# Banded attention and a leaky-relu MLP on one core: attention's products from the third batch on use TensorE's array in quarters, in one stretch a visit

## The chip, the core and the metric

The kernel runs on one core of a Trainium2 chip. The metric is the device time of one execution in microseconds (us). TensorE (PE) multiplies matrices into PSUM, which has eight banks of 512 fp32 columns on 128 rows; VectorE (DVE), ScalarE (ACT) and GpSimd (POOL) work on what is there and in SBUF; SyncE (SP) issues the loads.

## The reference

Attention over 8 batches, 8 heads, 576 tokens and 64 elements a head; heads 0 to 3 look back over 32 neighbours, heads 4 to 7 over 32 tokens at a distance of 4. Its output, as 4608 rows of 512, goes through an MLP:

```python
rel = pos[:, None] - pos[None, :]
mask_plain = (rel >= 0) & (rel < 32)
mask_dil = (rel >= 0) & (rel < 32 * 4) & (rel % 4 == 0)
scores = np.where(masks, q @ k.T / np.sqrt(64), -1e9)
attn = exp(scores - max); attn = attn / (attn.sum(-1) + 1e-9)
x = (attn @ v).transpose(0, 2, 1, 3).reshape(4608, 512)
h = x @ w_in                      # w_in is 512 x 2048
out = np.maximum(0.01 * h, h) @ w_out   # w_out is 2048 x 512
```

Inputs and the output are float32; the kernel's matrix operands are fp16.

## The kernel before

**The order of the work.** The kernel first lists tasks, each with an engine (or several to choose from), a duration, what it depends on and a priority. A planner lays them out engine by engine, goes backward over the result eight times to set priorities, and then adds to the priorities a table of numbers by task (NUDGE) and fixes some engines by hand (HAND). The instructions are emitted in the order that comes out. So a change to the tasks moves instructions on every engine, and what a row of an engine waits for is what the emitted order makes of it: each engine works through its own instructions in order, and semaphores hold one back until what it needs on another engine is done.

**Loading.** Query and key come in fp32, are cast to fp16 and turned, so that the 64 elements of a head lie on rows; two heads fill the 128 rows. Batches 0 and 1 (EARLY) are turned by TensorE (`turn`, L743, and `turn_rest` for the last 64 tokens) into PSUM and copied out. Batches 2 to 7 are turned by VectorE in 32x32 blocks (L708 to L735) into `turned`, and copied from there into `slots` by GpSimd, ScalarE or VectorE (`move`, L516 and L517).

**Attention.** A visit is a batch and a pair of heads; the order of pairs is VISITS = (2, 3, 0, 1), where 0 and 1 are plain and 2 and 3 are dilated. The keys of the two heads are interleaved on the 128 rows. A visit has two `unit`s. A unit is: scores, five products on the whole array (L899); Exp on ScalarE (L907); the mask as a multiply on VectorE (L911); from some batch on an add of overlapping parts (L932); sums of the exponentials, products with a block of ones (L924); values, five products (L918); 1/sum as Ln and Exp(-1 x) on ScalarE (L943, L945); and the multiply of values by it into `xt` on VectorE (L956). Scores, sums and values of a unit are three separate tasks of TensorE, and the order puts blocks of the MLP between them.

**The MLP.** `up` (L1057) makes one block of the hidden layer for 384 tokens, four products of 128x384 into one of the banks hps0 and hps1, and ScalarE's Prelu (L1073) takes it out. `up_pair` (L1091) does so for 192 tokens. The last three chunks of tokens use `ups7` (L1191), a scheme of seven products for eight. `down` (L1271) makes the first four output tiles; `group` (L1361, blocks of eight products 128x256, with sums on VectorE, L1347) makes the rest by seven products for eight, in the banks fps0, fps1 and tp, with evictions L1390 and L1392.

**PSUM.** Eight tiles of one bank each: tp, ops0, ops1, hps0, hps1, sps, fps0, fps1. An instruction on one bank is ordered only against what uses that bank.

Of the kernel before, what the change touches and what calls it, by code (L numbers as in the profile page):

```python
# [14 lines left out]
WIN = 32  # L15
# [3 lines left out]
WHEN = (3.92, 2.82, 39.64, 80.18, 115.4, 117.81, 161.72, 152.03)  # L19
# [3 lines left out]
ADDED = (2, 9)  # L23
LAPS = ("DVE", "POOL")
# [1643 lines left out]
```

## Time and profile before

| | before |
|---|---|
| median of 3 runs | 294.49 us (294.41 to 294.5) |
| span of the profiled execution | 292.5 us |
| time of the profiled execution beside its span | not listed |
| TensorE busy in the span | 285.2 us, 97% |
| VectorE, ScalarE, GpSimd busy | 226.8, 218.9, 121.2 us |
| share of TensorE in the chain that ended last | 93% |

A row of instructions reads: line, engine, operation, output and inputs, shape, then times in us. A group's row gives the count, the sum of the busy time in us and the mean of one in ns, then the idle time of the engine ahead of the group and what ended it. The records of TensorE overlap: a product's record lasts until its result is in PSUM, and the next one begins before that, so the time that a product costs is the spacing of the products, not the record.

### The profile page before, as it was taken

To read this page: it belongs to the slowest core of one execution; us is meant where nothing else is said; L and a number is where in the kernel's file an instruction comes from. 1 tells how busy PE (TensorE), PEld (TensorE's weight loads), DVE (VectorE), ACT (ScalarE), POOL (GpSimd) and SP (SyncE) were. 2 spreads that over 40 slices of the span, in tenths; PEclk is the share of its full clock that TensorE was granted. 3 is DMA by queue.
4 is the path that set the end of the run, shared out by engine and by line. 5 is a ranking of instruction groups with operands and counts; after the bars stand their busy time and mean duration, and the time that the engine had idled before them with its cause. 6 is when DMAs were issued, how large, how long until landed. Compare 5 with 4: busy or idle time off the path is not lost.

```text
span 292.5 us, 7626 instructions
## 1 busy us (share of the span) xinstructions
PE 285.2 (97%) x2924; PEld 226.4 (77%) x2924; DVE 226.8 (78%) x437; ACT 218.9 (75%) x483; POOL 121.2 (41%) x173
## 2 busy tenths in 40 slices
PE   6899999999999999999999999999999999999995
PEld 2567776776787788677777877887688999999985
DVE  7877588674799789858839889897878889678672
ACT  3997987589869966878888987888767966755522
POOL 5420452458537746964873774653425000000000
PEclk9999999999999999999999999999999999999999
DMA  7999999799898959999799798751101210121133
GB/s 244 267 389 396 395 377 224 150 168 218 142 188 185 179 144 174 191 168 208 197 170 160 180 205 151 195 134 59 36 2 36 75 38 0 38 74 36 38 109 110
DMA packets 156068, 47.15 MB, mean 161 GB/s; under 512 B 136832, under 2 KB 153344, under 8 KB 156032
## 3 DMA queue, kind: packets, MB, share of 16 engines
q1 hardware_dynamic: 155344, 46.04, 65.0%
q10 hardware_dynamic: 688, 0.63, 0.6%
q8 instruction: 23, 0.38, 0.5%
q14 instruction: 13, 0.11, 0.1%
HBM read 37.22 MB, written 9.44 MB: 160 GB/s over the span
## 4 chain that ended last, share of the span: by engine, by line
PE 93%; ACT 2%; DVE 2%; DMA 1%; issue 1%; ACTq 0%; DVEq 0%
PE hps L1057 27%; PE fps L1361 23%; PE tp L1361 9%; PE hps L1191 5%; PE fps L1271 4%; PE hps L1091 4%; PE ops L1191 3%; PE ops L918 3%; PE ops L899 2%; PE sps L899 2%; PE ops L924 2%; PE sps L1191 1%; DMA con<-consts 1%; PE sps L924 1%; PE ops L1361 1%; PE sps L918 1%
## 5 line engine op out<-in xcount | busy, mean ns | idle before, releaser
L1057 PE MATMUL hps<-xt,w_in 128*128 128x384 f16 x488 | 94.7, 325 | 0.0
L1361 PEld LDWEIGHTS <-gt 128*128 128x128 f16 x768 | 73.0, 98 | 9.8 <-DVE gt L1347 0.2
L1073 ACT ACTIVATE gt<-hps 128x384 f16<-128x384 f32 x122 | 59.1, 487 | 13.7 <-PE hps L1057 12.7
L1057 PEld LDWEIGHTS <-w_in 128*128 128x128 f16 x512 | 44.9, 98 | 21.3 <-issue 0.3
L505 POOL CAST slots<-vst 128x576 f16<-128x576 f32 x55 | 46.0, 861 | 22.7 <-DMA vst<-in_v_dram 5.6
L505 POOL CAST nat<-stg 128x576 f16<-128x576 f32 (+1 forms) x52 | 34.6, 687 | 48.6 <-DVE gt L1347 15.1
L1361 PE MATMUL fps<-w_out,gt 128*128 128x256 f16 x368 | 46.7, 272 | 0.0
L911 DVE TENSOR_TENSOR ee<-ee,con 128x384 f16<-128x384 f16 (+1 forms) x48 | 20.6, 430 | 15.3 <-ACT ee L907 14.9
L945 ACT ACTIVATE rc<-rc 128x288 f32<-128x288 f32 (+1 forms) x64 | 27.2, 436 | 1.1
L956 DVE TENSOR_TENSOR xt<-ops,rc 128x288 f16<-128x288 f32 (+2 forms) x44 | 19.3, 445 | 9.7 <-ACT rc L945 4.9
L516 ACT COPY slots<-turned 64x512 f16<-64x512 f16 (+1 forms) x30 | 23.8, 799 | 0.8 <-DVE turned L708 0.5
L1214 ACT ACTIVATE gt<-vst 128x384 f16<-128x384 f32 (+1 forms) x24 | 16.0, 684 | 8.0 <-DVE vst L1210 8.0
L899 PEld LDWEIGHTS <-slots 128*128 128x128 f16 x308 | 18.1, 98 | 4.7 <-DVE slots L517 0.4
L517 POOL COPY slots<-turned 64x576 f16<-64x576 f16 (+2 forms) x25 | 16.7, 675 | 11.2 <-ACT slots L516 3.5
L907 ACT ACTIVATE ee<-ops 128x416 f16<-128x416 f32 (+2 forms) x35 | 16.7, 487 | 3.6 <-PE ops L899 3.0
L918 PEld LDWEIGHTS <-slots 128*128 128x128 f16 x308 | 17.1, 97 | 2.8 <-ACT slots L504 0.6
L924 PEld LDWEIGHTS <-con 128*128 128x128 f16 x168 | 14.0, 97 | 5.9 <-issue 0.8
L708 DVE STREAM_TRANSPOSE turned<-nat 128x576 f16<-128x576 f16 x24 | 18.0, 759 | 0.1
L1390 ACT COPY stg<-fps 128x512 f32<-128x512 f32 (+1 forms) x20 | 10.4, 519 | 9.4 <-PE fps L1361 9.1
L907 ACT ACTIVATE ee<-sps 128x416 f16<-128x416 f32 (+2 forms) x29 | 14.4, 495 | 3.8 <-PE sps L899 2.7
L1347 DVE TENSOR_TENSOR gt<-gt 128x1024 f16<-128x1024 f16 x21 | 16.6, 789 | 0.3 <-PE fps L1361 0.2
L1191 PEld LDWEIGHTS <-w_in 128*128 128x128 f16 x192 | 16.2, 98 | 0.2
(158 smaller groups left out, 559.8 us busy)
## 6 DMA issues: line engine op xcount, KB each, us to landing
out_dram<-osb SPq DMA_DIRECT2D x32, 256.0 KB, 2.6
stg<-in_k_dram SPq DMA_DIRECT2D x48, 144.0 KB, 3.6
stg<-in_q_dram SPq DMA_DIRECT2D x48, 144.0 KB, 3.4
vst<-in_v_dram SPq DMA_DIRECT2D x16, 288.0 KB, 4.3
vst<-in_v_dram SPq DMA_DIRECT2D x32, 128.0 KB, 3.2
gt<-in_moe_w_in_dram SPq DMA_DIRECT2D x6, 512.0 KB, 6.8
stg<-in_q_dram SPq DMA_DIRECT2D x3, 512.0 KB, 6.9
stg<-in_k_dram SPq DMA_DIRECT2D x3, 512.0 KB, 9.1
```

The lines of the kernel that those rows point to most:

```text
L505: return ENG[e].tensor_copy(out=dst, in_=src)
L516: return nc.scalar.copy(out=dst, in_=src)
L899: nc.tensor.matmul(p_bank[:, c:c + w], slot(tn, KB + 128 * s, 0, 128, [1, 128]), slot(tn, qx, 0, 128, *qd), start=first or not by_pe, stop ...
L907: lambda e: nc.scalar.activation(out=et[:, 0:n], in_=p_bank[:, 0:n], func=AF.Exp, scale=SCALE), prio)
L911: lambda e: nc.vector.tensor_tensor(out=et[:, 0:n], in0=et[:, 0:n], in1=con[:, table:table + n], op=ALU.mult), prio,
L918: nc.tensor.matmul(at(dst, 0, 128, o, *od), lhs(s), et[:, c:c + w], start=i == 0, stop=i == len(steps) - 1, skip_group_check=True)
L924: nc.tensor.matmul(at(p_bank, 0, 128, o, *od), block_ones, at(et, 0, 128, c, *cd), start=i == 0, stop=i == len(rows) - 1, skip_group_check ...
L945: lambda e: nc.scalar.activation(out=rt, in_=rt, func=AF.Exp, scale=-1.0), prio)
L1057: nc.tensor.matmul(ht[:, 0:n], at(w_in, 0, 128, vi * DFF + j // 2 * 256 + j % 2, [2, 128]), at(xt[m % 2], 0, 128, vi * 1152 + x0 + x, [1, n]),
L1073: lambda e: nc.scalar.activation(out=gt[c % NG][:, j * n_c + x:j * n_c + x + n], in_=ht[:, 0:n], func=AF.Prelu, alpha=0.01),
L1191: nc.tensor.matmul(bk[:, n * i:n * i + n], w(v, 2 * z + i), x(v), start=first and i == 0 and v == 0, stop=i == 1 and v == 1, skip_group_ch ...
L1361: nc.tensor.matmul(bk[:, x:x + HN], tl[:, off + j * step:off + j * step + 128], rhs(j), start=first and x == 0 and j == 0, stop=j == HJ - ...
```

## The change

From the third batch (number 2) on, attention is made of bursts. A `burst(now, then, prio, lent)` is one task of TensorE: the sums and values of the visit `now`, then the scores of the next visit `then`. Every product uses a quarter of the array, 64 rows by 64 columns (`tile_position`); a step is four of them, one for each quarter, and the two row halves write different banks. A burst has four banks, `seats`: ops0, ops1, a lent one, and sps. The lent one is tp until the first `group` is made, then fps0 or fps1, by the roles that the groups so far leave to the two. There are 25 bursts, with 64 to 68 products each where both parts are present: 480 for scores, 480 for sums and 624 for values, in place of 612 on the whole array.

Behind a burst stand one Ln over ops1 and sps (576 columns, L1276) and one Exp(-1 x) (L1279) for the visit `now`; two multiplies into `xt` (L1293), the first of 128 columns over ops0 and the lent bank, the second of 448 over ops1 and sps; and for the visit `then` one Exp over ops0 and the lent bank (L1304; 2 x 448 or 2 x 384 columns) and one mask multiply (L1313). For such accesses to two banks PSUM is now one tile, `psum`, of 4096 columns, cut into the banks 0 to 7: tp, ops0, ops1, sps, hps0, hps1, fps0, fps1. `up` is now L1336 with its Prelu at L1352, and a product of `group` is L1639.

Other parts: batch 2 is loaded like the early ones and turned by TensorE (PACKED = 3; 36 products in the banks sps and ops0, L890 and L951); batches 3 to 7 are turned by VectorE straight into `slots`, keys no longer interleaved, so the copies out of `turned` are gone; the overlap adds are gone; the table of masks is smaller; the first of the last three chunks uses the same ring of banks as the other two; bursts are placed every 5.2 up blocks (PLACE, PACE); NUDGE now has a number for nearly every task, and HAND is longer.

Instructions before and after: TensorE 5850 and 7870 rows with weight loads, VectorE 438 and 374, ScalarE 487 and 345, GpSimd 177 and 115, SyncE 231 and 257.

```diff
-WHEN = (3.92, 2.82, 39.64, 80.18, 115.4, 117.81, 161.72, 152.03)
+WHEN = (3.92, 2.82)
-ADDED = (2, 9)
-LAPS = ("DVE", "POOL")
+PLACE = 4.0
+PACE = 5.2
+SWITCH = 0.2
...
-    EARLY = 2
+    EARLY, PACKED = 2, 3
...
-    def bank(name, dt=FP32):
-        return ps.tile([128, 512 if dt == FP32 else 1024], dt, name=name)
...
-    tpb = bank("tp", FP16)
-    tp32 = tpb.bitcast(FP32)
-    ops = [bank(f"ops{i}") for i in range(2)]
-    hps = [bank(f"hps{i}") for i in range(2)]
-    sps = bank("sps0")
-    fps = [bank(f"fps{i}") for i in range(2)]
+    psum = ps.tile([128, 4096], FP32, name="psum")
+    tp32, *ops, sps, hps0, hps1, fps0, fps1 = (psum[:, 512 * i:512 * i + 512] for i in range(8))
+    tpb, hps, fps = tp32.bitcast(FP16), [hps0, hps1], [fps0, fps1]
...
-        if b >= EARLY:
-            xn, x_old = ring("X", NX, x_users := [])
-            xk = turned[xn][:, 0:S]
-            tk = add("DVE", 0.68, [c_qk[1]] + x_old,
...
+        if b >= PACKED:
...
+            for o, x in ((0, 0), (1, KB)):
+                order = ([1, 144], [144, 4]) if dil and o == 0 else ([1, S],)
+                got.append(add("DVE", 0.68, [c_qk[o]] + old,
+                               lambda e, o=o, x=x, order=order: nc.vector.transpose(
+                                   slot(tn, x, 0, 128, *order), na[:, o * S:o * S + S]), prio))
+            n_users += got
+            q_ready[b, vi], k_ready[b, vi] = got[:1], got[1:]
...
+            q_bank = second_turn[vi] if b < EARLY else sps
...
-        summed = [t_m, t_e, t_id]
-        if added:
-            c0, d0, c1, d1, w = lap
-
...
+    def burst(now, then, prio, lent):
+
+        seats = [ops[0], ops[1], lent, sps]
+        room, mine = {}, {}
+        for bk in seats:
+            room[key(bk)], mine[key(bk)] = grab(bk)
+        if now is None:
+            for bk in seats[1::2]:
+                mine[key(bk)] += room[key(bk)]
+        jobs, deps, cols = [], sum(room.values(), []), 0
...
+        def product(bk, x, od, lhs, rhs, p, q, first, last):
+            p0, p1, q0, q1 = quarter(p, q)
+            jobs.append(lambda: nc.tensor.matmul(
+                at(bk, q0, q1, x, *od), lhs(p0, p1, q), rhs(p0, p1), start=first, stop=last,
+                skip_group_check=True, tile_position=(p0, q0)))
+
...
+            for n, two in enumerate(list(zip(sums_of(vi, 0), sums_of(vi, 1)))
+                                    + list(zip(values_of(vi, 0), values_of(vi, 1)))):
+                for p, (blk, c, w, dims, x, *part) in enumerate(two):
+                    if not part:
+                        bk, x, first = seats[2 * p + 1], 224 + x, n == 0
+                    elif part[0]:
+                        bk, x, first = seats[2 * p], 448 + x, part[0] == 1
+                    else:
+                        bk, first = seats[2 * p + 1], False
+
+                    def lhs(p0, p1, q, blk=blk, part=part):
+                        if not part:
+                            return con[p0:p1, M_ONE:M_ONE + 64]
+                        return slot(tn, VB + 128 * blk + 64 * q, p0, p1, [1, 64])
+
+                    for q in range(2):
+                        def rhs(p0, p1, q=q, c=c, w=w):
+                            o = 896 * en + 448 * q + c
+                            return e_all[p0:p1, o:o + w]
+                        product(bk, x, dims, lhs, rhs, p, q, first, True)
+            cols += 2 * (416 if vi < 2 else 384) + 30
+            deps = deps + [t_m, t_con[0]] + v_in[b, vi]
+        if then is not None:
...
+            for _, c, w, keys, asks in places(b2, v2):
+                for p in range(2):
+                    for q in range(2):
+                        def lhs(p0, p1, _, k=keys[q]):
+                            return slot(t2, KB + k[1], p0, p1, k[0])
+
+                        def rhs(p0, p1, a=asks[q]):
+                            return slot(t2, a[1], p0, p1, *a[0])
+                        product(seats[2 * p], c, [[1, w]], lhs, rhs, p, q, True, True)
...
+        t_b = add("PE", SWITCH + cols / 2400.0, deps, pe, prio, 0.0, "B")
...
+            t_l = add("ACT", 0.07 + S / 1200.0, [t_b] + r_old,
+                      lambda e: nc.scalar.activation(out=at(rt, 0, 128, 0, [288, 2], [1, 288]),
+                                                     in_=both(1, 224, None, [1, 288]), func=AF.Ln), prio)
+            t_r = add("ACT", 0.105 + S / 1200.0, [t_l],
+                      lambda e: nc.scalar.activation(out=rt, in_=rt, func=AF.Exp, scale=-1.0), prio)
+            x, xm = vi * 1152 + b % 2 * S, xt[b // 2 % 2]
...
+                    args = (at(xm, 0, 128, x + n0, [288, 2], [1, w]), both(i, 0 if i else 448, None, [1, w]),
+                            at(rt, 0, 128, n0, [288, 2], [1, w]))
...
+            for i, bk in enumerate(seats):
+                mine[key(bk)] += [t_l, ts[1]] if i % 2 else [ts[0]]
...
+        t_e = add("ACT", 0.07 + 2 * n / 1200.0, [t_b] + then[4][0],
+                  lambda e: nc.scalar.activation(out=at(et, 0, 128, 0, [448, 2], [1, n]),
+                                                 in_=bass.AP(tensor=seats[0].tensor, offset=seats[0].offset,
+                                                             ap=[list(seats[0].ap[0]), [
+                                                                 seats[2].offset - seats[0].offset, 2], [1, n]]),
+                                                 func=AF.Exp, scale=SCALE), prio)
+        mine[key(ops[0])].append(t_e)
...
-            ring5 = five if c > 9 else [hps[0], hps[1], ops[1]]
-            X, Y, Z = (ring5[(five_at[0] + i) % len(ring5)] for i in range(3))
+            X, Y, Z = (five[(five_at[0] + i) % len(five)] for i in range(3))
...
+    visits = [(b, vi) for b in range(EARLY, B) for vi in VISITS]
+    flow, lent = [0, None], [tp32]
+
+    def bursts(upto, prio):
+        while flow[0] <= len(visits) and PLACE + PACE * flow[0] <= upto:
+            k, then = flow[0], None
+            if k < len(visits):
...
+            flow[:] = k + 1, burst(flow[1], then, prio, lent[0])
...
+                lent[0] = trio[roles[0]]
```

What the order makes of it, first on TensorE, before, in the middle of the run. L918 are a unit's values, L1057 the blocks of `up`, L924 the unit's sums:

```order
L918 LDWEIGHTS slots [waits Pool_49]
L918 MATMUL sps_104<-ee_81,slots 128x96 [waits DVE_49]
...
L918 MATMUL sps_104<-ee_81,slots 128x2x16
L1057 LDWEIGHTS w_in
L1057 MATMUL hps_103<-xt_87,w_in 128x384 [waits Activation_49]
...
L1057 MATMUL hps_102<-xt_87,w_in 128x384 [waits Activation_49]
...
L924 LDWEIGHTS con
L924 MATMUL ops_101<-ee_81,con 128x2x96
```

Values stand ahead of two blocks of `up`, the sums behind them; each block waits for the Prelu that frees its own bank. On TensorE, after, the end of a burst (its last product is a score, 64x96), the `up` block behind it, and the first product of a `group`, which writes fps0:

```order
L1218 MATMUL psum<-slots 64x96
L1336 LDWEIGHTS w_in
L1336 MATMUL psum<-xt_79,w_in 128x384 [waits Activation_49]
L1336 LDWEIGHTS w_in
L1336 MATMUL psum<-xt_79,w_in 128x384
...
L1639 LDWEIGHTS pair_87
L1639 MATMUL psum<-wst_88,pair_87 128x256 [waits Activation_49]
L1639 LDWEIGHTS pair_87
L1639 MATMUL psum<-wst_88,pair_87 128x256
```

Sums, values and scores are now one stretch. The group's first product waits for ScalarE; it is the wide Exp (L1304) that stands first in the last piece below, which reads ops0 and fps1 and not fps0. On ScalarE, before, in the same part of the program, with Exps L907 of one bank, Prelus L1073, an eviction L1390 and the Ln and Exp(-1 x) of a unit:

```order
L907 ACTIVATE ee_81<-sps_104 128x416 [waits DVE_49,PE_49]
L1073 ACTIVATE gt_88<-hps_103 128x384 [waits PE_49]
L907 ACTIVATE ee_82<-ops_101 128x416 [waits DVE_49,PE_49]
L1390 COPY osb_91<-fps_105 128x512 [waits DMAHW6_49,PE_49]
L943 ACTIVATE rc_83<-sps_104 128x288 [waits PE_49]
L945 ACTIVATE rc_83<-rc_83 128x288 [waits Activation_49]
```

and after, with the wide Exp, the wide Ln and Exp(-1 x), and Prelus L1352:

```order
L1304 ACTIVATE ee<-psum 128x896 [waits DVE_49,PE_49]
L1352 ACTIVATE gt_80<-psum 128x384
L1276 ACTIVATE rc<-psum 128x576
L1668 COPY stg_68<-psum 128x512 [waits DMAHW0_49,DMAHW7_49,PE_49,Pool_49]
L1352 ACTIVATE gt_80<-psum 128x384 [waits PE_49]
L1279 ACTIVATE rc<-rc 128x576 [waits Activation_49]
```

This wide Exp reads ops0 and fps1. Of TensorE it waits for the last product of the `up` block behind the burst, the fourth L1336 of the piece above, which writes hps1; the Prelu behind the Exp waits for nothing more.

More of the change, by code (lines that the diff above doesn't have):

```diff
@@ L758, in turn @@
         after_q, after_k = ([tq], [tk]) if b == 0 else ([tq, tk], [tq, tk])
+        if b >= EARLY:
+            got = []
+            for o in range(2):
+                if not dil:
+                    dst = slot(tn, KB * o, 0, 128, [4, 128], [1, 4])
+                    src = at(bq, 0, 128, 512 * o, [1, 128], [128, 4])
+                else:
+                    dst = slot(tn, KB * o, 0, 128, [128 if o else 144, 4], [1, 128])
+                    src = at(bq, 0, 128, 512 * o, [128, 4], [1, 128])
+                got.append(move(dst, src, 512, after_q + old, prio, ("DVE", "ACT"), dil, bank_q))
+            q_users += got
+            q_ready[b, vi], k_ready[b, vi] = got[:1], got[1:]
+            return
         if dil:
@@ L826, in unit @@
         qr, kr = q_ready[b, vi], k_ready[b, vi]
-        added, nq, bias = b >= ADDED[dil], 288, []
+        nq, bias = 288, []
         if dil:
-            wide, run = ((96, 64), 128) if by_pe else ((96, 80), 144)
-            nq, n, steps = 2 * run, 2 * sum(wide) + 32 * (not by_pe), []
+            wide, run = (96, 64), 128
+            nq, n, steps = 2 * run, 2 * sum(wide), []
             for ab in range(2):
@@ L908, in unit @@
                                                  scale=SCALE), prio)
-        t_m = t_e if by_pe else add(
-            "DVE", 0.08 + n * 0.00052, [t_e, t_con[0]],
-            lambda e: nc.vector.tensor_tensor(out=et[:, 0:n], in0=et[:, 0:n],
-                                              in1=con[:, table:table + n], op=ALU.mult), prio,
-            lock=True)
         def second(dst, lhs):
@@ L1516, in attend @@
         else:
-            banks = dict.fromkeys(VISITS, [sps, ops[0]] if b == 7 and 9 in SEVEN else three)
+            banks = dict.fromkeys(VISITS, three)
         for n, vi in enumerate(VISITS):
@@ L1525 @@
     wide_banks = {2: fps[0], 3: fps[1], 4: tp32, 5: sps, 6: ops[0], 7: ops[1]}
+    visits = [(b, vi) for b in range(EARLY, B) for vi in VISITS]
[4 more added lines that the diff above has]
+            if k < len(visits):
+                b, vi = visits[k]
+                if vi == VISITS[0]:
+                    fetch(b, prio, 6.5)
+                if b < PACKED:
+                    if vi == VISITS[0]:
+                        turn_rest(b, prio)
+                    turn(b, vi, prio)
+                elif vi == VISITS[0]:
+                    for v in VISITS:
+                        turn(b, v, prio)
+                then = take(b, vi)
+            flow[:] = k + 1, burst(flow[1], then, prio, lent[0])
     def ups(c, x, n, batches, js=(0, NJ)):
@@ L1529, in ups @@
             for j in range(*js, 2):
+                if x:
+                    bursts(8 + j / 2, begins[c] + j * 1.3)
                 up_pair(c, j, x, n, batches, all_acts[c], hps[h_at[0] % 2])
@@ L1533, in ups @@
         for j in range(*js):
+            if c > 1:
+                bursts(16 * (c - 1) + j, begins[c] + j * 1.3)
             wide_j = c == 0 and j in wide_banks
@@ L1580 @@
             weight_sums()
-            half_free[0] = raw[0, "rest"][1] + raw[1, "rest"][1]
+            half_free[0] = raw[PACKED - 1, "rest"][1]
             part_free[0] = part_free[1] = rings["STG"][-1]
-        while n_g < len(groups) and groups[n_g][-1][0] < 3 * m + 3:
-            four = groups[n_g]
-            group(four, all_acts, begins[four[-1][0] + 1] + four[-1][1] * 2.0, n_g == len(groups) - 1)
-            n_g += 1
+        for c, batches in ((3 * m, [e]), (3 * m + 1, [e, o]), (3 * m + 2, [o])):
+            if c in SEVEN:
+                if c == SEVEN[0]:
+                    bursts(1e9, begins[c])
+                    in_sums()
+                ups7(c, batches, all_acts[c])
+            elif m:
+                ups(c, 0, 384, batches)
+            elif c == 2:
+                ups(2, 0, 384, [o])
+            while n_g < len(groups) and groups[n_g][-1][0] <= c and c > 1:
+                four = groups[n_g]
+                group(four, all_acts, begins[four[-1][0] + 1] + four[-1][1] * 2.0, n_g == len(groups) - 1)
+                lent[0] = trio[roles[0]]
+                n_g += 1
     order = plan.run()
@@ L1592 @@
     order.sort(key=lambda t: (t.start, t.n))
-    slow = next(t for t in order if t.eng == "POOL" and t.kind == "cast" and t in ups_at[0].deps)
+    slow = next((t for t in order if t.eng == "POOL" and t.kind == "cast" and t in ups_at[0].deps), None)
     kept = [t for t in order if t.eng == "ACT" and t.start < ups_at[1].start]
-    if slow.start < kept[-1].start:
+    if slow is not None and slow.start < kept[-1].start:
         slow.eng, slow.start = "ACT", kept[-1].start + 1e-4
```

309 lines of the change are left out of this document (174 added, 135 removed), and 294 rows, old and new, of the table NUDGE.

## The prediction

> **What bounds the kernel now.** I read the page first, then busy time by stretches, then the chain of work in the middle of the run, then groups of instructions by shape, and last the order of time where one engine hands to another. From the page:
>
> ```profile
> span 292.5 us, 7626 instructions
> ...
> PE 285.2 (97%) x2924; PEld 226.4 (77%) x2924; DVE 226.8 (78%) x437; ACT 218.9 (75%) x483; POOL 121.2 (41%) x173
> ...
> PE 93%; ACT 2%; DVE 2%; DMA 1%; issue 1%; ACTq 0%; DVEq 0%
> ```
>
> Stretches, with columns length, then busy time and count of TensorE, its weight loads, VectorE, ScalarE and GpSimd, then the granted clock:
>
> ```profile
> 0.00:16.00 16.00, 12.27 (x97) 6.83 (x98) 12.72 (x22) 10.84 (x23) 7.81 (x16) 1.00 0.89 261
> ...
> 87.75:117.00 29.25, 29.25 (x303) 23.29 (x302) 24.72 (x47) 23.58 (x53) 19.27 (x29) 1.00 0.86 170
> 175.50:204.75 29.25, 29.25 (x297) 22.98 (x295) 25.75 (x47) 24.52 (x55) 14.30 (x20) 1.00 0.58 135
> ```
>
> TensorE is the bound, and without slack: in the two middle stretches it is busy for all 29.25 us at a clock of 1.00, while no other engine passes 25.8. So each microsecond of work taken from TensorE shortens the run, each microsecond for which it stands still lengthens it, and the other engines matter only through the moments at which they let TensorE go on. The three timed runs have a median of 294.49 us; the profiled execution's own whole time is not listed. The median stands 2.0 us over its span; I take those 2.0 us as what lies around the span, unchanged, and set the differences below on 294.5. Under 0.2% (0.6 us) a measurement of this kernel can't tell from no change.
>
> **What attention costs TensorE before.** The chain of work from 142 to 152 us shows its pieces (start, time until TensorE could go on, line):
>
> ```profile
> 142.42 0.38 PE ops L899 x10
> 142.80 1.30 PE hps L1057 x8
> ...
> 145.16 0.66 PE hps L1057 x4
> 145.82 0.14 PE ops L924 x3
> ...
> 146.61 0.12 PE ops L924 x2
> 146.73 0.87 PE fps L1361 x8
> 147.61 0.19 PE ops L918 x5
> ...
> 150.80 0.17 PE ops L899 x5
> ...
> 151.63 0.17 PE sps L924 x3
> 151.80 0.18 PE ops L918 x5
> ```
>
> A visit is two units. A plain visit costs 0.38 for its two sets of scores, 0.19 + 0.18 for values and 0.14 + 0.12 for sums: 1.01 us. A dilated one costs twice 0.17 + 0.18 + 0.17: 1.04 us. Batches 2 to 7 have 12 visits of each kind, 12 x 1.01 + 12 x 1.04 = 24.6 us. This is all that the quarters can work on.
>
> **The products in quarters: 24.6 becomes 14.0, between 14.0 and 56.** No row shows a product on a quarter of the array. From below: the four products of a step run side by side, and a step costs what a whole-array product of the same width costs now. Sums, values and scores then take one pass of five steps a visit instead of two, and the values one or two short steps more. Short steps, from the order of time:
>
> ```profile
> 21.74 0.53 PE L997 MATMUL sps<-slots 128*128 128x16 f16 x14
> ```
>
> These 14 end 0.53 after the first begins; one is recorded at about 0.18, so the others follow at (0.53 - 0.18)/13 = 0.027. A plain visit is then 3 x 0.19 + 0.03 = 0.60, a dilated one 3 x 0.17 + 0.06 = 0.57, 24 of them 14.0 us. From above: nothing overlaps, four times as much, 56 us. I take 14.0, since the four products of a step stand next to each other, read and write different quarters, and the two row halves write different banks. The Trainium skill (TensorEngine Tiling (Array Packing), Key Properties) says that different tiles can load weights and multiply in parallel; no run shows that yet.
>
> **Changing the division: +5.0, between 0 and 8.** Each of the 25 bursts has whole-array products before and behind it, so the division changes 50 times. The nearest rows are the recorded time of a product against its spacing:
>
> ```profile
> L1057 PE MATMUL hps<-xt,w_in 128*128 128x384 f16 x448 | 86.1, 325 | 0.0
> ...
> L918 PE MATMUL ops<-ee,slots 128*128 128x96 f16 x108 | 11.0, 205 | 0.0
> ```
>
> A 96-wide product is recorded at 205 ns, and its five stand 0.04 apart, so 0.16 us passes between the moment when the next can follow and its end. A change costs between nothing and this, 0 to 8 us in all; with no nearer row I take 0.1, 5.0 us. The Trainium skill (same page and section) says that a change of tiling mode drains TensorE. By that rule it would be the whole 8, and the sum 3 us more.
>
> **Batch 2 turned by TensorE: +2.0.** 36 products of 128x128 are added. Four of these (L743) are recorded as 0.38 where one is about 0.22, so one takes (0.38 - 0.22)/3 = 0.055:
>
> ```profile
> 15.71 0.38 PE L743 MATMUL fps<-con,nat 128*128 128x128 f16 x4 [0.23 <-DVE slots L517]
> ```
>
> 36 x 0.055 = 2.0. TensorE's own work thus goes from 24.6 to 14.0 + 5.0 + 2.0 = 21.0: **-3.6 us**, between -8.6 (no cost of division) and, with that at 8, -0.6.
>
> **The wait that comes with it.** Before, scores, sums and values lie in eight separate bank tiles, and an instruction waits only for its own bank. Now PSUM is one tile, and an access to two banks is ordered against everything between its first and its last column. The wide Exp (L1304) reads ops0, bank 1, with the lent bank. In 6 of 24 bursts that is tp, bank 0, its neighbour; in 18 it is fps0 or fps1, bank 6 or 7, and between lie the hps banks that the up projection writes. In the new order an up block of four products follows the burst. The wide Exp then waits for that block as well, though it reads nothing of it, and the next block that writes a bank in the box waits for the Exp. The same goes for the first multiply (L1293), which reads ops0 and the lent bank. So TensorE, which had a slot of other work for each wait, stops. What a stop costs comes from these rows:
>
> ```profile
> 140.96 1.46 PE L1057 MATMUL hps<-xt,w_in 128*128 128x384 f16 x8
> 142.46 0.49 ACT L1073 ACTIVATE gt<-hps 128x384 f16<-128x384 f32 x1 [0.16 <-PE hps L1057]
> ```
> ```profile
> 13.70 0.86 ACT L504 CAST slots<-vst 128x576 f16<-128x576 f32 x1
> 14.62 0.32 PE L918 MATMUL ops<-ee,slots 128*128 128x96 f16 x4 [0.22 <-ACT slots L504]
> ```
> ```profile
> L1073 ACT ACTIVATE gt<-hps 128x384 f16<-128x384 f32 x122 | 59.1, 487 | 13.7 <-PE hps L1057 12.7
> ...
> L907 ACT ACTIVATE ee<-ops 128x320 f16<-128x320 f32 x8 | 3.5, 437 | 0.4 <-PE ops L899 0.4
> ...
> L1015 ACT ACTIVATE ee<-ops 128x448 f16<-128x448 f32 x1 | 0.5, 543 | 1.9 <-PE ops L997 1.9
> ```
> ```profile
> L1032 DVE TENSOR_TENSOR xt<-ops,rc 128x128 f16<-128x128 f32 x4 | 1.2, 329 | 2.5 <-ACT rc L1026 2.5
> ```
>
> A product of 384 is recorded at 325 ns, but its four take 0.66, 0.164 each: TensorE could go on 0.16 us before the end of the record. ScalarE starts 0.04 after that end (140.96 + 1.46 = 142.42, start 142.46), and TensorE 0.06 after ScalarE's (13.70 + 0.86 = 14.56, start 14.62). An Exp grows from 437 to 543 ns over 128 columns, 0.83 ns each, so 896 columns take 0.543 + 448 x 0.00083 = 0.915 and 768 take 0.81. A stop for an Exp is 0.16 + 0.04 + 0.915 + 0.06 = 1.18 us at 896 columns, 1.07 at 768. The first multiply of 128 columns takes 0.329, a stop for it 0.16 + 0.04 + 0.33 + 0.06 = 0.59.
>
> How often: I went along the new order, burst by burst, asking which TensorE block waits and what stands between the awaited block and it. For the Exp nine stops are bare, with nothing between: 5 x 1.18 + 4 x 1.07 = 10.2 us. In three a block of eight products (0.87, the chain's row at 146.73) lies between, 0.3 left each, 0.9; three more keep about 0.7, 2.1; the last three are covered. That is 13.2 us. For the first multiply about nine are bare, 9 x 0.59 = 5.3; two in which ScalarE comes late to its Ln leave 0.8 and 1.2, and partly covered ones about 1.4, in all 8.7 us. Together **+21.9**, with the bare ones alone, 15.5, as the lower end; above, I allow 1.3 times, 28.5, since ScalarE and VectorE have other work in their queues (a Prelu of 487 ns, for one) when an awaited instruction comes.
>
> **What costs nothing.** VectorE issues fewer instructions (438 to 374), ScalarE (487 to 345) and GpSimd (177 to 115): overlap adds, copies behind turning and half of the Exp, Ln and Exp(-1) instructions go. All of it lies beside a TensorE that never waits in the middle stretches, so none of it shortens the run; were TensorE's cover gone, these engines have 25.8 us of work in 29.25 at most. Loads in another order on SP's queue and the start: TensorE's first 16 us hold 3.7 us without work, which bounds a gain; a slip of one step there I put at 1 us, and take 0. The seven-product chunks that use other banks issue the same products: 0.
>
> **Sum.** -3.6 + 21.9 = +18.3: 294.5 + 18.3 = **312.8 us**. Lower end: -8.6 + 15.5 - 3.7 = +3.2, 297.7. Upper end: -0.6 + 28.5 + 1 = +28.9, 323.4, and with the weights of the next part in question 326.
>
> **The rivals.**
>
> *The waits cost nothing that matters, and it is faster.* If the wide Exp is released by the burst's last product rather than by the up block behind it, it runs beside that block of 0.66; a bare stop falls from 1.18 to 0.52, one for a multiply to nothing. With a division that is free: -8.6 + 9 x 0.52 = -3.9, 290.6 us. For it speaks that the block behind each burst is there to cover just this; against it that the order has the Exp waiting for a TensorE instruction that stands behind the up block. It decides if the Exp starts less than 0.5 us after the burst's last product: then all stops together come below 8.6, the most that TensorE's work can shrink. Chance 0.08.
>
> *Weight loads are no longer hidden.* A quarter has its own weights, 64 to 68 loads a burst against 25 or 26 a visit before (612 in 24 visits).
>
> ```profile
> L899 PEld LDWEIGHTS <-slots x308: 95/98/99, 8.5 to 231.8; 128*128 128x128 f16 x154
> ```
>
> A load of 128 columns is recorded at 98 ns while products follow at 0.036; if a load of 64 takes half, 0.049, and the four quarters load side by side but not under the products before, a step takes 0.049 instead of 0.036, and 16 steps in 24 visits add 16 x 24 x 0.013 = 5.0 us: 317.8. For it speaks that the two rates are close; against it that before, loads twice as wide hide. Chance 0.12. The Trainium skill (TensorEngine Tiling (Array Packing), Gotcha 2) says that column tiling excludes Fast Weight Load. By its TensorE: Matmul & The Clock Gate, LDWEIGHTS, 64 columns at 1.2 per ns would take 53 ns, an estimate that gives 1.5 us more than the sum above.
>
> *The quarters take turns.* If each product is issued no faster than the short ones above, 0.027 us, the four of a step take 0.108 instead of 0.036: 24 visits of 65 products are 42 us instead of 14.0, 28 more, 341 us. For it speaks that this is the closest spacing that the trace shows anywhere; against it that those 14 products all use the same rows and columns of the array. Without any overlap it would be 56, and 355 us. Chance 0.06.
>
> *Saving and stops cancel* within 0.6 us, with a free division and few stops: chance 0.02.
>
> **How the numbers follow.** The forecast keeps 0.72, and is the likeliest: 312.8 us. The range, 297.5 to 326, holds the forecast with its bounds and the rival on weight loads; it leaves out the faster one, the cancelling one and the one in which quarters take turns, 0.16. Faster has 0.08, same 0.02, and slower 0.72 + 0.12 + 0.06 = 0.90.
>
> **What would show it.** Right: in the profile after, TensorE is no longer busy for whole middle stretches; idle TensorE time of 15 to 28 us lies before up and down blocks, ended by ScalarE at L1304 and VectorE at L1293, and the wide Exp starts about 0.2 us after an up block could have been followed, not after the burst. A burst with scores, sums and values takes about 0.6 us, 0.8 with its two changes. Bursts of 1.7 us or more would show quarters taking turns; a pause of over 0.16 at a burst's ends a dearer change of division. The forecast is wrong if TensorE's idle time stays under 9 us, or if the bursts with their changes take as long as the 24.6 us that they replace.

## The result, and the profile after

The changed kernel takes **404.81 us** (median of 4 runs, 404.0 to 406.89) against 294.45 us before (294.3 to 294.5): a ratio of 1.376, with a 95% interval of 1.373 to 1.380. That is slower by 110 us, where 18 were forecast, and outside the range of 297.5 to 326. Times are medians of a kernel's runs; for two kernels below, the slowest of four runs, in a slower state, is left out. The page after:

```profile
span 402.7 us, 9407 instructions
...
PE 307.1 (76%) x3934; PEld 228.7 (57%) x3934; DVE 225.3 (56%) x376; ACT 190.8 (47%) x385; POOL 76.4 (19%) x110
...
PEclk8785565856599998999899998999999999999999
...
GB/s 244 143 53 53 54 53 52 125 126 126 237 289 265 160 197 163 137 158 164 125 163 143 142 155 111 134 132 137 163 87 55 2 28 54 28 2 55 53 93 92
...
PE 54%; SPq 18%; DVE 9%; DMA 9%; ACT 5%; issue 3%; DVEq 0%; ACTq 0%
```

TensorE fell from 97% to 76% busy, and SyncE's queue, which had no place in the chain before, now has 18% of it. Five slices of 10 us each, from 20 to 70 us, move 52 to 54 GB/s. The same as busy time by stretches, with columns as in the prediction and the DMA share and GB/s last:

```profile
0.00:40.00 40.00, 21.56 (x185) 13.57 (x185) 16.02 (x30) 15.31 (x36) 9.56 (x19) 0.76 0.39 124
40.00:80.00 40.00, 11.89 (x78) 7.23 (x75) 1.96 (x6) 6.66 (x16) 3.21 (x5) 0.63 0.19 67
80.00:120.00 40.00, 20.72 (x167) 14.68 (x168) 12.30 (x28) 13.90 (x32) 8.44 (x14) 0.67 0.63 196
120.00:200.00 80.00, 72.20 (x1076) 50.47 (x1075) 56.75 (x93) 44.96 (x92) 20.41 (x30) 0.96 0.83 173
200.00:340.00 140.00, 121.59 (x1825) 87.52 (x1823) 92.77 (x133) 75.38 (x141) 34.81 (x43) 0.99 0.52 109
```

TensorE stands idle for 66 us in the first 120, with every other engine idler still, and for 26 us from 120 to 340 us. The second number is about what the prediction is on; the first is not in it. What the first 120 us wait for is in the waits (waiter, whom it waits for, total us, times, longest):

```profile
POOL w_in L655 <- DMA gt<-in_moe_w_in_dram: 57.0, 4, 20.1
...
DVE w_in L655 <- DMA gt<-in_moe_w_in_dram: 40.1, 4, 16.1
DVE w_in L655 <- DMA wst<-in_moe_w_in_dram: 31.0, 2, 20.0
```

and in the order of time on SyncE's queue:

```profile
12.93 39.75 SPq L639 DMA_DIRECT2D gt<-in_moe_w_in_dram  x6
52.73 9.78 SPq L639 DMA_DIRECT2D wst<-in_moe_w_in_dram  x1
62.62 9.68 SPq L639 DMA_DIRECT2D stg<-in_q_dram  x1
72.42 5.64 SPq L639 DMA_DIRECT2D stg<-in_k_dram  x1
78.11 5.60 SPq L639 DMA_DIRECT2D wst<-in_moe_w_in_dram  x1
```

The first weights, w_in, trickle in for 70 us, and the queue is held behind them; every other load waits in turn. The diff has one line on them that its core above leaves out and that the prediction doesn't name; its only words on loads are "Loads in another order on SP's queue". In this line the source of each load counted 64 rows and then 2 heads before, and counts 2 heads and then 64 rows now, since quarters want the two heads' rows one after the other and not interleaved:

```diff
-            src = dram(moe_w_in, heads_of(vi)[0] * D * DFF + x, [DFF, 64], [2 * D * DFF, 2], [1, 1024])
+            src = dram(moe_w_in, heads_of(vi)[0] * D * DFF + x, [2 * D * DFF, 2], [DFF, 64], [1, 1024])
```

A stretch in which little but these loads moves:

```profile
25.00:50.00 25.00, 7.51 (x71) 5.16 (x72) 2.64 (x7) 3.04 (x8) 2.04 (x3) 0.56 0.13 53
```

The DMA share is 0.13, about 2 of 16 engines, as many as the outermost count of the source. The Trainium skill (DMA: Bandwidth & Descriptors, Why a DMA increments its semaphore by 16 and not by 1) states just this rule: the number of engines is the largest up to 16 that divides the slowest dimension of both sides. The trace agrees, with a share of 0.13 and 53 GB/s.

### The profile page after: what moved, and what is told of

Its sections match the earlier page's. It is cut to its first block, busy times and chain, and to the rows that moved or that the text cites. A ratio compares the mean times of both kernels' runs of the same rounds, so it can differ in the third digit from the quotient of the medians.

```text
span 402.7 us, 9407 instructions
## 1 busy us (share of the span) xinstructions
PE 307.1 (76%) x3934; PEld 228.7 (57%) x3934; DVE 225.3 (56%) x376; ACT 190.8 (47%) x385; POOL 76.4 (19%) x110
## 4 chain that ended last, share of the span: by engine, by line
PE 54%; SPq 18%; DVE 9%; DMA 9%; ACT 5%; issue 3%; DVEq 0%; ACTq 0%
PE psum L1639 21%; SPq L639 18%; PE psum L1336 16%; PE psum L1469 7%; DMA wst<-in_moe_w_in_dram 6%; DVE slots L881 4%; PE psum L1218 4%; ACT ee L1304 3%; PE psum L1549 3%; DVE xt L1293 3%; DMA stg<-in_k_dram 2%; DMA vst<-in_v_dram 1%; PE psum L1370 1%; ACT gt L1352 1%; DVE ee L1313 1%
## 5 line engine op out<-in xcount | busy, mean ns | idle before, releaser
L1336 PE MATMUL psum<-xt,w_in 128*128 128x384 f16 x512 | 108.3, 345 | 59.6 <-DVE w_in L655 17.5
L1336 PEld LDWEIGHTS <-w_in 128*128 128x128 f16 x512 | 50.0, 102 | 94.4 <-issue 42.3
L1352 ACT ACTIVATE gt<-psum 128x384 f16<-128x384 f32 x128 | 61.3, 491 | 73.0 <-PE psum L1336 57.8
L1639 PEld LDWEIGHTS <-gt 128*128 128x128 f16 x768 | 76.0, 100 | 15.7 <-issue 2.0
L1639 PE MATMUL psum<-w_out,gt 128*128 128x256 f16 x512 | 65.1, 276 | 0.9 <-DVE xt L1293 0.9
L881 DVE STREAM_TRANSPOSE slots<-nat 128x576 f16<-128x576 f16 x40 | 47.7, 1245 | 1.1 <-POOL nat L655 1.1
L1293 DVE TENSOR_TENSOR xt<-psum,rc 128x448 f16<-128x448 f32 (+1 forms) x48 | 24.8, 542 | 25.9 <-PE psum L1639 10.4
L655 POOL CAST slots<-vst 128x640 f16<-128x640 f32 (+1 forms) x33 | 23.6, 735 | 50.7 <-DVE ee L1313 21.3
L1313 DVE TENSOR_TENSOR ee<-ee,con 128x768 f16<-128x768 f16 (+1 forms) x24 | 14.8, 617 | 26.8 <-ACT ee L1304 26.7
L1304 ACT ACTIVATE ee<-psum 128x768 f16<-128x768 f32 (+1 forms) x24 | 20.7, 863 | 18.4 <-PE psum L1336 11.5
L890 PE MATMUL psum<-con,nat 128*128 128x128 f16 x96 | 11.0, 264 | 18.9 <-DVE nat L655 15.3
L1488 DVE TENSOR_TENSOR vst<-psum,vst 128x384 f32<-128x384 f32 x36 | 19.2, 552 | 4.1 <-PE psum L1469 2.2
L890 PEld LDWEIGHTS <-nat 128*128 128x128 f16 x96 | 8.6, 121 | 22.3 <-DVE nat L655 15.8
L667 DVE COPY slots<-psum 128x512 f16<-128x512 f16 (+3 forms) x31 | 15.6, 527 | 7.5 <-PE psum L890 6.3
L1639 PE MATMUL psum<-t,gt 128*128 128x256 f16 x128 | 17.7, 290 | 0.0
L1383 ACT ACTIVATE gt<-psum 128x384 f16<-128x384 f32 x16 | 7.8, 491 | 20.8 <-PE psum L1370 20.7
L1057 ACT ACTIVATE rc<-psum 128x256 f32<-128x256 f32 (+2 forms) x16 | 5.7, 385 | 24.4 <-PE psum L1047 24.3
```

The lines of the kernel that those rows point to most:

```text
L655: return ENG[e].tensor_copy(out=dst, in_=src)
L881: lambda e, o=o, x=x, order=order: nc.vector.transpose(slot(tn, x, 0, 128, *order), na[:, o * S:o * S + S]), prio))
L890: nc.tensor.transpose(bk[:, c + t * 128:c + t * 128 + 128], na[:, off + t * 128:off + t * 128 + 128], ident)
L1293: lambda e, args=args: nc.vector.tensor_tensor(out=args[0], in0=args[1], in1=args[2], op=ALU.mult), prio))
L1304: lambda e: nc.scalar.activation(out=at(et, 0, 128, 0, [448, 2], [1, n]), in_=bass.AP(tensor=seats[0].tensor, offset=seats[0].offset, ap=[ ...
L1313: lambda e: nc.vector.tensor_tensor(out=at(et, 0, 128, 0, [448, 2], [1, n]), in0=at(et, 0, 128, 0, [448, 2], [1, n]), in1=at(con, 0, 128, ...
```

## The experiments

**Loads.** Theory L: the trickle costs most of the 110 us. Rival Q: the quarters and the clock do.

```diff
-                     lambda e: eng.dma_start(dst, src), prio,
+                     lambda e: [eng.dma_start(dst[64 * h:64 * h + 64], s) for h, s in enumerate(src)]
+                     if isinstance(src, list) else eng.dma_start(dst, src), prio,
...
-            src = dram(moe_w_in, heads_of(vi)[0] * D * DFF + x, [2 * D * DFF, 2], [DFF, 64], [1, 1024])
+            src = [dram(moe_w_in, (heads_of(vi)[0] + 2 * h) * D * DFF + x, [DFF, 64], [1, 1024]) for h in range(2)]
```

> The changed kernel, with each load of w_in as two loads of 64 rows, one for each head, in place of one whose source counts 2 heads outermost and then 64 rows. Theory L (loads): in the profile after, from 13 to 84 us little but w_in moves, at 52 to 59 GB/s and a DMA share of about 0.12, or 2 of 16 engines; 8 loads of 0.52 MB at 53 GB/s are 79 us, where before they moved at some 380 GB/s, 11 us. With the source 64 rows outermost they should be fast again, at least 68 us go, and what is left is what was forecast without them: 313 to 325 us, with a granted clock of 1.0 from 20 us on. Rival Q (quarters): the added time is from the quarters and from the lower clock (0.6 to 0.8 granted up to 120 us) that pauses bring; then this kernel stays above 380 us.

Measured: **340.98 us** (339.38 to 342.1), ratio to before 1.156 [1.152, 1.161]: 63.8 us less than the changed kernel, where at least 68 were expected. Rival Q falls; the value is 16 above the upper end expected, so more is left than was forecast.

The same line by itself in the kernel before (`[DFF, 64], [2 * D * DFF, 2]` exchanged):

> The kernel before, with the source of w_in's loads counted as after: 2 heads outermost, then 64 rows. The rows of w_in then stand in another order than x's, so the up projection multiplies the wrong rows; nothing else changes. Theory L: w_in's eight loads take 79 us in place of 11, and the kernel takes 68 to 95 us more, 362 to 390 us. Theory Q: as before, 294.5 us, within 3.

Measured: **365.57 us**, ratio 1.241 [1.237, 1.246], 70.9 us more, without a single quarter and inside the 68 to 95 of theory L. Its first 80 us show what the changed kernel's do:

```profile
0.00:40.00 40.00, 20.31 (x186) 12.38 (x187) 15.97 (x29) 17.49 (x39) 8.68 (x17) 0.79 0.39 125
40.00:80.00 40.00, 10.21 (x59) 5.94 (x59) 4.91 (x14) 3.42 (x8) 0.87 (x1) 0.57 0.21 75
```

**False waits.** Theory W: the boxes over banks in between make TensorE stop. Rival T: it would have to stop for the banks themselves. The edit, on top of the two loads, only moves the banks, so that fps0, ops0 and fps1 lie side by side:

```diff
-    tp32, *ops, sps, hps0, hps1, fps0, fps1 = (psum[:, 512 * i:512 * i + 512] for i in range(8))
+    tp32, *ops, sps, hps0, hps1, fps0, fps1 = (psum[:, 512 * i:512 * i + 512] for i in (0, 2, 4, 5, 6, 7, 1, 3))
```

> As the one with two loads, and the eight banks lie in another order within the one PSUM tile: tp, fps0, ops0, fps1, ops1, sps, hps0, hps1, so that the lent bank is ops0's neighbour whether it is fps0 or fps1. Nothing else changes. Theory W (false waits): TensorE's waits for L1304 (9.9 us) and L1293 (14.1 us from 137 to 340 us) in the profile after come from boxes over the banks between; this takes most of the waits out of the program (of 35 waits of TensorE on banks that it doesn't touch, 6 are left), and the time falls by 12 to 24 us against the kernel with two loads. Rival T (true waits): TensorE would have to wait for the same Exp and multiply for the banks themselves, and the time falls by less than 5 us.

Measured: **319.94 us**, ratio 1.085 [1.081, 1.090], 21.0 us less than with two loads alone, on the same chip. (Later kernels ran on two other chips; the kernel before takes 294.4 to 294.7 on each.) The waits of TensorE of the kernel with two loads:

```profile
PE psum L1337 <- ACT ee L1305: 7.9, 9, 1.7
PE psum L1337 <- DVE xt L1294: 5.3, 6, 2.8
PE psum L1219 <- DVE xt L1294: 4.6, 3, 2.2
PE psum L891 <- DVE xt L1294: 4.4, 2, 3.3
...
PE psum L1640 <- ACT ee L1305: 2.0, 2, 1.0
```

and with the other order of banks (lines are one further than in the changed kernel):

```profile
PE psum L1219 <- DVE xt L1294: 5.0, 3, 2.2
PE psum L891 <- DVE xt L1294: 4.1, 2, 2.8
PE psum L1640 <- DVE xt L1294: 2.6, 1, 2.6
...
PE psum L1640 <- ACT ee L1305: 0.4, 1, 0.4
```

No `up` block (L1337) waits for the wide Exp or the first multiply any more. Theory W stands, rival T falls. What is left are waits of bursts, turns and a group for multiplies: 11.7 us in all, against 15.7 with two loads alone.

Splitting the wide Exp in two, one bank each, in place of moving the banks:

```diff
...
+                  lambda e: [nc.scalar.activation(out=et[:, 448 * i:448 * i + n], in_=seats[2 * i][:, 0:n],
+                                                  func=AF.Exp, scale=SCALE) for i in range(2)], prio)
```

> As the one with two loads, and the wide Exp is two Exps, one for ops0 and one for the lent bank; the first multiply over two banks stays. Theory W: TensorE's waits for L1304 go, 9.9 us, less up to 24 x 0.1 where ScalarE is on the path: 7 to 10 us under the kernel with two loads, with the waits for L1293 left. Theory T: within 3 us of it.

Measured: 331.58 us (330.35 to 333.69), ratio 1.126 [1.120, 1.132], 9.4 us under the kernel with two loads, as expected. In its trace TensorE no longer waits for an Exp of a burst.

And one tile in the kernel before, with no access over two banks:

> The kernel before, with the eight banks as slices of one PSUM tile in the order of after; every instruction uses one bank still. Theory W: one tile costs nothing as long as no access spans banks: within 1 us of 294.5. Rival: a tile as large as PSUM makes instructions on different banks wait for each other, and it is slower by 5 us or more.

Measured: 294.09 us, ratio 0.999 [0.997, 1.000]. The one tile costs nothing by itself.

**What is left of the start.** Two loads of 64 rows mended the engines' number, yet TensorE idled 11.3 us in the first 40 us. With one load of 128 rows again, counted as before:

> The kernel with two loads and the other order of banks, but w_in in one load of 128 rows again, counted as before (64 rows outermost, then the 2 heads). The rows of w_in then stand in another order than x's, so the up projection multiplies the wrong rows; nothing else changes. Theory H (half the rows): two loads of 64 rows move at 241 to 273 GB/s from 20 to 40 us with the DMA engines busy throughout, where the kernel before moves 394 to 401, and TensorE idles 11.3 us in the first 40 us against 4.0; besides the clock is 0.84 from 40 to 60 us, 3 us. The time falls by 7 to 11 us from 319.9. Rival B2: batch 2's own loads and turns are what fills the start; it falls by less than 3 us.

Measured: 312.47 us (308.99 to 313.04), ratio 1.058 [1.052, 1.064], 7.5 less than with the other order of banks. The stretch from 20 to 40 us, in the kernel with the other order of banks, in this one, and in the kernel before:

```profile
20.00:40.00 20.00, 13.44 (x146) 9.27 (x144) 6.20 (x17) 9.22 (x24) 3.98 (x6) 0.99 1.05 257
```
```profile
20.00:40.00 20.00, 18.84 (x198) 13.60 (x197) 13.18 (x29) 15.23 (x37) 9.41 (x15) 1.00 1.01 363
```
```profile
20.00:40.00 20.00, 20.00 (x218) 14.71 (x217) 13.87 (x32) 17.55 (x41) 5.80 (x10) 1.00 1.05 397
```

The DMA engines are busy throughout in all three, and move 257, 363 and 397 GB/s; TensorE idles 6.6, 1.2 and 0.0 us. Theory H (half the rows) against N (number of loads), in the kernel before, first with the halves one after the other:

> The kernel before, with each load of w_in as two loads of 64 rows, the first head's into rows 0 to 63 and the second's into rows 64 to 127 (the rows of w_in then stand in another order than x's, so the up projection multiplies the wrong rows). Theory H (half the rows): loads that write 64 neighbouring rows move at about 250 GB/s; 4.2 MB then take 17 us in place of 11, and the kernel takes 4 to 9 us more than 294.5. Rival N (number): it isn't the rows but that there are twice as many loads of half the size; then this kernel and the one with every second row are slower alike. Rival B2 (batch 2 fills the start): both stay within 1 us.

Measured: 301.2 us, ratio 1.024 [1.021, 1.028], 6.8 us more. Then with every second row (`every2(dst, h, 0, [1, 1024])` for the destination):

> The kernel before, with each load of w_in as two loads of 64 rows, each into every second row, so that w_in stands as it did. Theory H: within 1.5 us of 294.5. Rival N: 4 to 9 us more, as with halves.

Measured: 296.63 us, ratio 1.008 [1.005, 1.010], 2.2 us more. Both expected values are missed: H alone allowed 1.5 us here, N alone at least 4. So H has about two thirds of the 6.8 and N, or the issue of eight more loads, about one third. Issuing the second half from ScalarE's queue:

> The kernel with two loads and the other order of banks, with the second head's load of each pair issued by ScalarE's queue in place of SyncE's, so that loads into the lower and the upper 64 rows can run at the same time. If theory H holds because loads into the same 64 rows follow each other, it falls by 4 to 10 us from 319.9; if ScalarE, busy 84% from 10 to 20 us, is held up by eight more issues, it rises by up to 5.

Measured: 323.64 us (320.45 to 324.1), ratio 1.095 [1.089, 1.102], 3.7 more than 319.94. Running both halves at once doesn't speed them up: from 14 to 28 us loads of both queues were in flight together and moved 222 GB/s (in the one trace, of the slowest run), against 244 from SyncE's queue alone, with the DMA engines busy throughout in both. Whether the 3.7 us are ScalarE's issues isn't settled.

**The turns on VectorE.** Of the 40 turns that write `slots` directly, the ten of dilated queries write in steps of 144 elements. One of each kind, from the order of time of the changed kernel:

```profile
213.21 0.77 DVE L881 STREAM_TRANSPOSE slots<-nat 128x576 f16<-128x576 f16 x1
...
239.97 2.65 DVE L881 STREAM_TRANSPOSE slots<-nat 128x576 f16<-128x576 f16 x1
```

Theory S: they make VectorE late for the multiplies. The edit is `order = ([1, S],)` for all.

> The kernel with two loads and the other order of banks, but VectorE writes the turned queries of dilated heads (batches 3 to 7) in their own order, not scattered over four residues; the scores of those visits then use the wrong tokens. Theory S (scatter): 10 of 40 turns (L882) take 2.8 us where the other 30 take 0.77, so VectorE comes late to the multiplies, and TensorE waits 12 us for L1294; the time falls by 8 to 12 us from 319.9. Rival O (order): the multiplies stand late in VectorE's row anyway; it falls by less than 3 us.

Measured: 316.02 us, ratio 1.072 [1.067, 1.076]: 3.9 less, where 8 to 12 were expected. TensorE's waits for the multiplies fall from 11.7 to 5.6 us, so the theory has the wait right and its size wrong by half or more. The same turns with GpSimd putting them in order, as before the change:

> The kernel with two loads and the other order of banks, and the queries of dilated heads (batches 3 to 7) are turned by VectorE into a buffer and put into the order of residues by a GpSimd copy, as before; the result is the reference's again. Theory S: VectorE is free of the ten turns of 2.8 us as in the kernel that leaves them unscattered (316.0 us), GpSimd stands idle three quarters of the time, so 314 to 318 us. Rival: the copies come late to the scores, 320 us or more.

Measured: 314.63 us (312.35 to 316.21), ratio 1.068 [1.061, 1.075]; the copies hide. It is the fastest version of the changed kernel here that computes all of the reference, and still 20 us slower than the kernel before.

One load of 128 rows and unscattered turns together:

> Both of these together (w_in in one load of 128 rows, turned queries in their own order; the results are wrong for both reasons). If both theories hold, and TensorE's work shrinks by the 3.6 us forecast, the start and the middle are as before and it takes 291 to 297 us; if only one holds 307 to 313; if neither 315 or more.

Measured: 306.22 us (305.15 to 307.97), ratio 1.040 [1.034, 1.045]: 6.3 less than with the one load, and 11.6 more than before. The forecast of 291 to 297 for this case missed. Its stretches up to 200 us, and then those of the kernel before:

```profile
0.00:40.00 40.00, 34.31 (x348) 22.87 (x349) 26.41 (x55) 28.86 (x68) 16.99 (x33) 1.00 0.95 319
40.00:80.00 40.00, 36.85 (x464) 25.36 (x465) 23.40 (x50) 22.48 (x55) 11.04 (x15) 0.92 0.94 230
80.00:200.00 120.00, 115.60 (x1856) 84.03 (x1849) 81.83 (x135) 76.64 (x145) 37.88 (x56) 1.00 0.84 165
```
```profile
0.00:40.00 40.00, 35.96 (x358) 24.10 (x359) 30.17 (x61) 31.75 (x72) 14.78 (x27) 1.00 0.98 343
40.00:80.00 40.00, 39.70 (x421) 28.28 (x419) 27.91 (x57) 31.97 (x74) 20.71 (x29) 1.00 0.94 197
80.00:200.00 120.00, 119.95 (x1212) 93.92 (x1210) 99.44 (x189) 98.00 (x218) 74.91 (x108) 1.00 0.87 177
```

From 40 to 80 and from 80 to 200 us TensorE idles 3.2 and 4.4 us, where before it idled 0.3 and 0.1. The clock of 0.92 over 40 us takes about 3 more (40 x 0.08, an estimate), and the first 40 us, with 5.7 us idle against 4.0, give 2 more.

## Why the prediction was wrong

Step by step from 404.8 us: the loads' engines 63.8, false waits 21.0, half-row loads 7.5, scattered turns 6.3 (3.9 by themselves), and 11.6 left over before. The two steps on loads are 71.3 us together, and the same line cost the kernel before 70.9.

**The step that failed** is in the paragraph on what costs nothing: "Loads in another order on SP's queue and the start", taken at 0 and bounded by 1 us above. What the runs showed in its place is 71 us. The line on w_in stood in the full diff; the prediction took loads for a matter of their order in the queue, and no load of w_in was priced. That there was nothing to hide a slower load behind could be read beforehand: in the kernel before, the DMA engines are busy throughout from 20 to 40 us (the third of the rows from 20 to 40 us above). That a source counted 2 outermost moves 53 GB/s is in no row of the kernel before. The bound of 1 us had no reason that excluded more; by it the range ended 79 us too low.

**Loads alone don't save the forecast.** Without the two steps on loads the account leaves 404.8 - 71.3 = 333.5 us, which no run has by itself: 21 above the forecast of 312.8, and outside the range as well. The stops are in it much as forecast. What is missing are the scattered turns (6.3), and 15.2 between the saving of 3.6 on TensorE and the 11.6 us that are left over.

**Stops.** The mechanism was right. The wide Exp, estimated at 0.915 us for 896 columns, is recorded at 0.92. A stop, in the changed kernel:

```profile
210.11 0.37 PE L1218 MATMUL psum<-ee,con 64*64 64x96 f16 x20
...
210.31 0.39 PE L1218 MATMUL psum<-ee,slots 64*64 64x32 f16 x28
210.54 0.38 PE L1218 MATMUL psum<-slots 64*64 64x64 f16 x20
...
210.85 0.82 PE L1336 MATMUL psum<-xt,w_in 128*128 128x384 f16 x4
...
211.71 0.92 ACT L1304 ACTIVATE ee<-psum 128x896 f16<-128x896 f32 x1 [1.01 <-PE psum L1336]
...
212.53 0.65 ACT L1276 ACTIVATE rc<-psum 128x576 f32<-128x576 f32 x1
...
212.68 0.81 PE L1336 MATMUL psum<-xt,w_in 128*128 128x384 f16 x4 [1.00 <-ACT ee L1304]
```

The burst is over at 210.85, the Exp waits for the `up` block behind it until 211.71, and the next block starts at 212.68. It could have gone on at 210.85 + 0.66 = 211.51: 1.17 us lost, 1.18 forecast. All stops: 21.9 forecast, 21.0 by the order of banks, so the rival that the waits cost nothing falls. Splitting the Exp alone gave 9.4 (13.2 forecast for the Exp), which leaves 11.6 for the rest (8.7 forecast). That the rest is the multiply's is not shown: with the banks moved, TensorE's waits named after the Exp fall from 9.9 to 0.4 us, those after multiplies only from 15.7 to 11.7. So 13.5 of the 21.0 us are waits seen in the traces. Part of the remaining 7.5 is the end of the record ahead of each stop (in the one shown, 1.00 of the 1.17 us lost is seen as a wait); no run takes the rest apart. The sum came out near, in part by luck. The 26 us of idle time from 120 to 340 us also fit the 15 to 28 of the prediction by luck: some 8 of them are waits of bursts and a turn for multiplies, not of `up` and `down` blocks as forecast.

**Quarters** run side by side: the 68 products above, from 210.11 to the next block at 210.85, take 0.74 us with their change of division. Taken from the start of every product in that trace, products of a burst stand 10 ns apart on average. A step of four with 96 columns takes 43 ns (median), and before, whole-array products of 96 columns stood 42 apart. The 25 bursts come to 15.7 us from first to last product, 16.7 with their last steps (14.0 forecast). Ahead of a burst 0.094 us are lost, behind it 0.135 to the next block (median), of which 0.04 is a step: 25 x (0.094 + 0.095) = 4.7 us for the division (5.0 forecast). With batch 2's 2.0 as forecast, which was not measured apart, this is 16.7 + 4.7 + 2.0 = 23.4 in place of 24.6: -1.2 us, not -3.6, a third of the saving. The rivals fall: quarters that take turns would stand 0.027 apart, and loads that don't hide would make a step 0.049. A quarter's load is recorded at 107 to 110 ns in the median, and still hides. The Trainium skill (TensorEngine Tiling (Array Packing), Key Properties) has a change of mode drain TensorE; the trace has a change at 0.09 us, a little over half of the 0.16 that a whole emptying was put at.

**VectorE's list** was counted in instructions, not in time. There are fewer of them, but ten turns at 2.7 us, and VectorE is busy for 225.3 us after against 226.8 before. That its list doesn't shorten the run was right; that it doesn't lengthen it was taken for granted, and was wrong by 4 to 6 us. ScalarE's 345 instructions are 385 in the trace. And the range's end of 326 isn't worked out: 323.4 with the 5.0 of the rival on weight loads would be 328.4.

**Left open** are the last 11.6 us, of the kernel with one load of 128 rows, moved banks and unscattered turns. Its span is 12.1 us longer than before, 9.5 of them idle TensorE, at the start and from 40 to 200 us. The order was laid out for other costs, and a load of keys that lands late heads one of the longest stops (3.1 us), but no run here takes that apart.

## What to carry to other kernels

A line of a diff that reorders an access pattern of a load is a change of its price: look at the outermost count on both sides and at which rows it writes, and price the load before calling it an order. In one PSUM tile, an access that spans two banks was ordered here against all that lies between; put banks that are read together side by side, which took one line here and was worth 21 us. An upper bound needs a reason that excludes more, as a term does; the smallest bound in the sum was the one that broke it.

## What the runs showed of the hardware that was not expected

- Loads whose source counts 2 outermost moved 52 to 54 GB/s, at a DMA share of 0.13.
- With half-row loads of w_in (64 neighbouring rows of SBUF) among the loads from 20 to 40 us, the DMA engines were as busy (share 1.05) as with loads of all 128 rows (1.01), and moved 257 GB/s against 363. Halves from two queues at once moved no more: 222 GB/s from 14 to 28 us.
- Products on 64x64 quarters, each with its own weights, followed each other at 10 ns on average, a step of four 96-wide ones at 43 ns, and a change between whole array and quarters took 0.09 us each way.
- A turn of 128x576 on VectorE took 0.77 us where it wrote its rows in order, and 2.57 to 2.85 us where it wrote in steps of 144 elements.
- While TensorE idled for want of weights, its granted clock fell to 0.63 (40 to 80 us), and in the kernel before with the same loads to 0.57.
